# 256 rows of a weight matrix loaded in blocks of 80 and 16 partitions, with two permutation matmuls

## The chip, the core and the metric

The kernel runs on one core of one Trainium2 chip. The metric is the device time of one execution in microseconds (us). Engines are named as in the profile: PE (TensorE matmul), PEld (TensorE weight load), DVE (VectorE), ACT (ScalarE), POOL (GpSimd), SP (SyncE, which issues nearly all transfers). Sixteen DMA engines move the data.

## The reference, cut to what matters

One token passes a grouped-query attention over a long cache and, beside it, a gated feed-forward block; a sigmoid gate mixes the two.

```python
q = x @ wq                                  # x: 512, wq: 512 x 4096, 32 heads of 128
p = softmax(q . k_cache * 128**-0.5)        # 8 groups of 4 heads, 32768 keys of 128
a = (p @ v_cache) @ wo                      # wo: 4096 x 512
b = (silu(x @ w_gate) * (x @ w_up)) @ w_down    # w_gate, w_up: 512 x 1792; w_down: 1792 x 512
g = sigmoid((x * gate_w).sum())
out = g * a + (1 - g) * b
```

The two caches are 134 of the 148 MB that the kernel reads (8 x 32768 x 128 x 2 bytes each); everything is bf16.

## The kernel before

**Transfers.** SP issues one list of transfers in a fixed order (lines 317 to 348): wq, x and gate_w, w_gate and w_up; then the caches in pages of 4 MB (a page is one half of one group's keys or values: 128 partitions, 32 KB each), into four page buffers, each issued as soon as its buffer is free (waits at lines 307 and 312); then w_down in one transfer of 128 partitions with 14 KB each (line 343, tile `wd`); then wo in five transfers (line 338), cut by `WO_CUTS = [0, 8, 18, 26, 30, 32]` into 8, 10, 8, 4 and 2 blocks of 128 rows. Each ends by raising a semaphore of its own by 16.

**Start.** PE turns x and gate_w into columns (line 357; DVE copies them at 570 and 571), makes q from wq (370), permutes it (381), and makes the two feed-forward products from w_gate and w_up (394): 14 columns (`FC = 14`) of 128 values for each, four matmuls per column, into columns of the PSUM tile `ps_m`. Column j, partition p is feature 14 p + j, so the weight is read with a step of 14 elements. ACT and DVE make of it `tT` (520, 609, 613): 128 x 14, feature 14 p + j at partition p, which is the order in which `wd` has the rows of w_down.

**Loop over the eight groups.** PE transposes K pages (408), DVE copies the result to SBUF (630), PE makes the scores (420), DVE their maxima (635), ACT the exponentials (535), PE the sums over values (465).

**End** (`emit_end`, lines 475 to 498, and 673 to 691). PE sums the exponentials' sums (477, into `ps_e`); DVE takes the reciprocal (653), scales it (655) and, through a matmul with a permutation (491), makes `O2`, the attention output as 32 columns (668). `emit_wide` (205) multiplies one column with one 128 x 512 block, into one of four rows of the PSUM tile `ps_w`: 8 blocks of w_down, then 8 of wo (the first cut), the other 6 of w_down, and 10 of wo (the second cut). DVE copies `ps_w` to `part` (685). `emit_rows` (217) adds the four rows of `part`, and the other 14 blocks of wo, in four matmuls of 128 columns each. DVE writes `res_row` (687), and two small stores on SP and ACT (244) end the kernel.

Of the kernel before, what the change touches and what calls it, by code (L numbers as in the profile page):

```python
# [8 lines left out]
BF16 = mybir.dt.bfloat16  # L9
# [4 lines left out]
def bass_gated_mix__gqa_block_cached__swiglu_ffn__decode_kernel(  # L14
# [17 lines left out]
    H = A_wq.shape[1] // DH  # L32
    HPG = H // G
    F = B_w_gate.shape[1]
# [1 line left out]
    assert DH == 128 and D % 128 == 0 and F % 128 == 0 and HPG == 4 and NOUT == 512  # L36
    assert H == 32 and G >= 2
    KC = D // 128
    FC = F // 128

    R = 128
    BLK = 128 * R
# [13 lines left out]
    SCALE = float(DH) ** -0.5  # L56
    assert UPG == STEP == 4 * HPG and UPP % NKT == 0 and UPP % NST == 0
    assert KC * H * DH <= PAGE and 2 * KC * F <= PAGE and WOJ * NOUT <= PAGE
    WO_CUTS = [0, 8, 18, 26, 30, 32]
    KW = 1  # L60
    WD_CUT = 8
    WIDE = WO_CUTS[KW + 1]
# [3 lines left out]
    NSTRIP = 4  # L66
# [10 lines left out]
    with ExitStack() as es:  # L77
# [8 lines left out]
        sem_ld_wd = S_("s_ld_wd")  # L86
# [7 lines left out]
        sem_ident = S_("s_ident")  # L94
# [8 lines left out]
        sem_dve_x = S_("s_dve_x")  # L103
# [4 lines left out]
        sem_dve_tT = S_("s_dve_tT")  # L108
# [21 lines left out]
        def T(name, shape, dt):  # L130
            return es.enter_context(nc.sbuf_tensor(name, shape, dt))
# [6 lines left out]
        ident_f = T("ident_f", [128, 128], FP32)  # L138
        perm = T("perm", [128, 2, 128], BF16)
        pmat = T("pmat", [128, 128], BF16)  # L140
        xT = T("xT", [128, KC], BF16)
        gwT = T("gwT", [128, KC], FP32)
        prod_col = T("prod_col", [128, KC], FP32)
# [7 lines left out]
        sg = T("sg", [128, FC], FP32)  # L151
        t1 = T("t1", [128, FC], FP32)
        tT = T("tT", [128, FC], BF16)
        wd = T("wd", [128, FC, NOUT], BF16)
        page = T("page", [128, NPG, PAGE], BF16)
        ktT = T("ktT", [128, NKT, 2 * UW], BF16)
# [15 lines left out]
        O2 = T("O2", [128, WOJ], BF16)  # L172
# [9 lines left out]
        ps_m = P("ps_m", [128, 512], FP32)  # L182
# [3 lines left out]
        M_G0 = M_Q0 + H  # L186
        M_U0 = M_G0 + FC
        M_O0 = M_U0 + FC
# [11 lines left out]
        wgu = page[:, PG_F, 0 : 2 * KC * F].rearrange("p (w c f) -> p w c f", w=2, c=KC)  # L200
        wo_v = page[:, PG_X, 0 : WOJ * NOUT].rearrange("p (j n) -> p j n", j=WOJ)

        def emit_wide(pe, w, vec, j, first, last):
            c = j % NSTRIP
            return pe.matmul(  # L205
                ps_w[32 * c : 32 * c + 1, :],
                vec[:, j : j + 1],
                w[:, j, :],
                start=first,
                stop=last,  # L210
                skip_group_check=True,
            )
# [14 lines left out]
        def emit_wo(pe, k):  # L227
            pe.wait_ge(sem_wo[k], 16)
            for j in range(WO_CUTS[k], WO_CUTS[k + 1]):
                if j < WIDE:  # L230
                    ins = emit_wide(pe, wo_v, O2, j, False, j >= WIDE - NSTRIP)
                else:
                    ins = emit_rows(
                        pe,
                        lambda e: O2[:, j : j + 1] if e else O2z[:, j - WIDE, :],
                        wo_v[:, j, :],
                        False,
                        j == WOJ - 1,
                    )
            return ins  # L240
# [8 lines left out]
        with nc.Block("main") as block:  # L249
            @block.gpsimd  # L250
            def _(pool):
                pool.memset(ones_bf[:, :], 1.0).then_inc(sem_const, 1)
                pool.memset(ones_f[:, :], 1.0).then_inc(sem_const, 1)
                npool = [0]

                def chain(ins):
                    ins.then_inc(sem_pool, 1)
                    npool[0] += 1
                    pool.wait_ge(sem_pool, npool[0])

                pool.load_library(library_config.all_libraries[1])

                def ones_where(t, base, pattern):
                    return pool.affine_select(
                        out=t,
                        in_=t,
                        compare_op=ALU.not_equal,
                        fill=1.0,
                        base=base,
                        pattern=pattern,  # L270
                        channel_multiplier=1,
                    )

                pool.memset(ident[:, :], 0.0)
                pool.memset(ident_f[:, :], 0.0)
                pool.memset(perm[:, :, :], 0.0)
                pool.memset(sel5[:, :], 0.0)
                chain(pool.memset(pmat[:, :], 0.0))
                ones_where(ident[:, :], 0, [[-1, 128]]).then_inc(sem_ident, 1)
                ones_where(ident_f[:, :], 0, [[-1, 128]]).then_inc(sem_ident, 1)  # L280
                for e in range(2):
                    ones_where(perm[:, e, :], -e, [[0, 2], [-2, 64]]).then_inc(sem_ident, 1)
                ones_where(pmat[:, :], 0, [[-1, 32], [-32, 4]]).then_inc(sem_ident, 1)
                for c in range(NSTRIP):
                    chain(ones_where(sel4, -32 * c, [[-1, 16]]))
                pool.sem_inc(sem_ident, 1)
                pool.wait_ge(sem_dve_gpart, 1)
                pool.partition_all_reduce(gtot[:, :], gpart[:, :], 128, ReduceOp.add).then_inc(
                    sem_gtot, 1
                )  # L290
                for g in range(G):
                    pool.wait_ge(sem_pmax, STEP * (g + 1))
                    pool.partition_all_reduce(  # L293
                        gmax[:, g, :], pmax[:, g * STEP : g * STEP + HPG], 128, ReduceOp.max
                    ).then_inc(sem_gmax, 1)

            @block.sync
            def _(sp):
# [36 lines left out]
                def load_wo(k):  # L335
# [4 lines left out]
                load_v(G - 1, 0)  # L340
                sp.wait_ge(sem_fill, UPG * (G - 1) + UPP)
                cache(A_v_cache, G - 1, 1, PG_K[0], sem_page[PG_K[0]])
                sp.dma_start(  # L343
                    wd[:, :, :], B_w_down.rearrange("(p j) n -> p j n", j=FC)
                ).then_inc(sem_ld_wd, 16)
                sp.wait_ge(sem_pe_q, 1)
                for k in range(len(sem_wo)):
                    load_wo(k)
# [2 lines left out]
            def _(pe):  # L351
# [10 lines left out]
                            stop=True,  # L362
                        )
                ins.then_inc(sem_pe_x, 1)
                pe.wait_ge(sem_dve_x, 2)

                pe.wait_ge(sem_q, 16)
                for h in range(H):
# [6 lines left out]
                            stop=(c == KC - 1),  # L375
                        )
                ins.then_inc(sem_pe_q, 1)
                pe.wait_ge(sem_ident, 6)
                pe.wait_ge(sem_dve_qT, 1)
                for e in range(2):  # L380
                    ins = pe.matmul(
# [9 lines left out]
                for w, base in enumerate((M_G0, M_U0)):  # L391
                    for j in range(FC):
                        for c in range(KC):
                            ins = pe.matmul(  # L394
                                ps_m[:, base + j : base + j + 1],
                                wgu[:, w, c, :].rearrange("d (p j) -> d j p", j=FC)[:, j, :],
                                xT[:, c : c + 1],
                                start=(c == 0),
                                stop=(c == KC - 1),
                            )  # L400
# [73 lines left out]

                def emit_end():
                    pe.wait_ge(sem_dve_esum2, 1)
                    pe.matmul(  # L477
                        ps_e[:, 0:H],
                        ones_f[:, :],
                        esum2[:, :, :].rearrange("p g h -> p (g h)"),  # L480
                        start=True,
                        stop=True,
                    ).then_inc(sem_pe_S, 1)
                    emit_reduce((G + 1) * STEP)
                    pe.wait_ge(sem_dve_tT, 1)
                    pe.wait_ge(sem_ld_wd, 16)
                    pe.wait_ge(sem_psw, 1)
                    for j in range(WD_CUT):
                        emit_wide(pe, wd, tT, j, j < NSTRIP, False)
                    pe.wait_ge(sem_dve_oT2, 1)  # L490
                    pe.matmul(
                        ps_m[:, M_O0 : M_O0 + WOJ], pmat[:, :], O2a[:, :], start=True, stop=True
                    ).then_inc(sem_pe_O2, 1)
                    pe.wait_ge(sem_dve_O2, 1)
                    for k in range(KW):
                        emit_wo(pe, k)
                    for j in range(WD_CUT, FC):
                        emit_wide(pe, wd, tT, j, False, False)

                with pe.Fori(0, (G + 1) * STEP, STEP) as i:  # L500
                    for b in range(NB):
# [56 lines left out]
            def _(dve):  # L558
# [8 lines left out]
                dchain(dve.memset(qblk[:, :], 0.0))  # L567
                dve.sem_inc(sem_rc, 2 * STEP)
                dve.wait_ge(sem_pe_x, 1)
                dve.tensor_copy(xT[:, :], ps_m[:, M_X0 : M_X0 + KC]).then_inc(sem_dve_x, 1)  # L570
                dve.tensor_copy(gwT[:, :], ps_m[:, M_X0 + KC : M_X0 + 2 * KC]).then_inc(
                    sem_dve_x, 1
                )
                dve.wait_ge(sem_dve_x, 2)
                dve.tensor_tensor(prod_col[:, :], xT[:, :], gwT[:, :], ALU.mult).then_inc(
                    sem_dve_prod, 1
                )
# [44 lines left out]
                def copy_red(i, at):  # L622
                    dve.wait_ge(sem_red, i)
                    dve.tensor_copy(oT[:, at], ps_m[:, M_P0 : M_P0 + HPG]).then_inc(sem_rc, STEP)

                with dve.Fori(0, G * STEP, STEP) as i:
# [27 lines left out]
                dchain(  # L654
                    dve.tensor_scalar(rSg[:, :], rS[:, :], g_col[:, 0:1], None, op0=ALU.mult)
                )
                copy_red((G + 1) * STEP, slice((G + 1) * STEP, (G + 1) * STEP + HPG))
                dve.wait_ge(sem_rc, STEP * (G + 2))
                dve.tensor_tensor(
# [60 lines left out]
```

## Time and profile before

| | us |
|---|---|
| median of 3 runs (lowest to highest) | 351.55 (351.51 to 351.67) |
| the profiled execution: its own time | 351.52 |
| the profiled execution: span from first to last instruction | 350.2 |

| engine | busy us | share of the span |
|---|---|---|
| PE | 269.0 | 77% |
| PEld | 230.9 | 66% |
| DVE | 176.8 | 50% |
| ACT | 32.3 | 9% |
| POOL | 6.9 | 2% |
| DMA, SP's queue (q1) | | 98.6% of 16 engines' span, 148.12 MB |

Times inside an execution are counted from the start of the span. The profile has, beside busy times, a row of 40 slices for each engine (a digit is the busy share in tenths), the chain of work that ended last, followed back from the last instruction, and the groups of instructions with the mean time of one. The trace also has a record of each DMA packet: its queue, start, duration and bytes, but not the number of the DMA engine that ran it.

### The profile page before, as it was taken

How to read it: one execution, taken by the hardware profiler on the slowest of the kernel's cores; microseconds unless marked ns; L12 is line 12 of the kernel's file. 1: busy time of each engine (PE TensorE's matmuls, PEld its weight loads, DVE VectorE, ACT ScalarE, POOL GpSimd, SP SyncE). 2: the span in 40 equal slices, each digit the busy share in tenths (PEclk: the TensorE clock that was granted, in tenths of full speed). 3: DMA queues.
4: the chain of work that ended last, by engine and by line, in shares of the span. 5: the costliest groups of instructions: out<-in, count | busy, mean ns of one | idle time of the engine just before them, and what ended most of it. 6: DMA issues, size and time to landing. Idle time of an engine off the chain costs nothing.

```text
span 350.2 us, 8919 instructions
## 1 busy us (share of the span) xinstructions
PE 269.0 (77%) x4005; PEld 230.9 (66%) x4005; DVE 176.8 (50%) x193; ACT 32.3 (9%) x148; POOL 6.9 (2%) x29
## 2 busy tenths in 40 slices
PE   0446987799999959897797969694896949795675
PEld 0446987787796939495785839392886849493332
DVE  0111868474783928366382828183473819184011
ACT  1000000500030040002100040004000040004000
POOL 4000000000000000000000000000000000000000
PEclk9999989696998989679696969899698969679565
DMA  8999999999999999999999999999999999999995
GB/s 348 395 453 417 438 445 425 418 419 449 434 430 423 427 446 430 430 423 423 449 430 434 419 434 438 434 430 419 442 438 434 423 423 442 438 434 419 425 415 234
DMA packets 5924, 148.23 MB, mean 423 GB/s; under 512 B 666, under 2 KB 668, under 8 KB 924
## 3 DMA queue, kind: packets, MB, share of 16 engines
q1 hardware_dynamic: 5912, 148.12, 98.6%
q8 instruction: 6, 0.10, 0.1%
q14 instruction: 2, 0.02, 0.0%
q10 hardware_dynamic: 4, 0.00, 0.0%
HBM read 148.11 MB, written 0.00 MB: 423 GB/s over the span
## 4 chain that ended last, share of the span: by engine, by line
DMA 64%; PE 32%; DVE 2%; SPq 1%; issue 1%
DMA page<-in_A_k_cache_dram 53%; PE pst L408 24%; DMA page<-in_A_wo_dram 11%; PE ps_sc L420 5%; DVE ktT L630 1%; PE ps_o L465 1%; PE pst L217 1%; PE pst L205 0%; PE ps_m L446 0%; SPq L321 0%; SPq L300 0%; DVE part L685 0%; SPq L343 0%; SPq L338 0%; SPq L317 0%
## 5 line engine op out<-in xcount | busy, mean ns | idle before, releaser
L630 DVE COPY ktT<-pst 128x2048 bf16<-128x2048 bf16 x128 | 156.1, 1224 | 106.4 <-PE pst L408 99.2
L408 PE MATMUL pst<-ident_f,page 128*128 128x128 f32 x1024 | 158.8, 313 | 40.9 <-DMA page<-in_A_k_cache_dram 35.6
L408 PEld LDWEIGHTS pst<-ident_f,page 128*128 128x128 f32 x1024 | 136.1, 163 | 51.6 <-DMA page<-in_A_k_cache_dram 43.7
L420 PE MATMUL ps_sc<-qcur,ktT 128*128 128x8 bf16 x2048 | 67.8, 166 | 8.6 <-DVE ktT L630 8.6
L420 PEld LDWEIGHTS ps_sc<-qcur,ktT 128*128 128x128 bf16 x2048 | 66.9, 97 | 11.3 <-DVE ktT L630 10.0
L465 PE MATMUL ps_o<-page,ET 128*16 128x512 bf16 x512 | 43.2, 497 | 4.6 <-DMA page<-in_A_v_cache_dram 4.6
L465 PEld LDWEIGHTS ps_o<-page,ET 128*16 128x16 bf16 x512 | 13.5, 105 | 23.8 <-issue 11.9
L526 ACT ACTIVATE nbias<-gmax 128x4 f32<-128x4 f32 x8 | 1.7, 207 | 263.4 <-POOL gmax L293 263.4
L535 ACT ACTIVATE ET<-ps_sc,nbias 128x128 bf16<-128x128 f32 x64 | 24.1, 553 | 0.6
L535 ACT ACTIVATION_READ_ACCUMULATOR ET<-ps_sc,nbias 128x1 f32 x64 | 18.0, 282 | 0.0
L635 DVE TENSOR_REDUCE pmaxf<-ps_sc 128x4 f32<-128x512 f32 x16 | 11.1, 692 | 11.5 <-PE ps_sc L420 11.5
L446 PE MATMUL ps_m<-sel,acc 128*128 128x4 f32 x72 | 10.4, 268 | 3.8 <-ACT acc L547 3.8
L446 PEld LDWEIGHTS ps_m<-sel,acc 128*128 128x128 f32 x72 | 9.8, 211 | 4.4 <-ACT acc L547 4.4
L394 PE MATMUL ps_m<-xT,page 128*128 128x1 bf16 x112 | 6.9, 198 | 5.0 <-DMA page<-in_B_w_up_dram 5.0
L357 PE MATMUL ps_m<-ones_bf,x_row 1*128 1x1 bf16 x4 | 0.3, 172 | 12.9 <-DMA gw_row<-in_gate_w_dram 12.9
L394 PEld LDWEIGHTS ps_m<-xT,page 128*128 128x128 bf16 x112 | 6.8, 159 | 5.1 <-DMA page<-in_B_w_up_dram 5.1
L293 POOL PARTITION_ALL_REDUCE gmax<-pmax x8 | 3.0, 373 | 302.8 <-DVE pmax L637 302.8
L357 PEld LDWEIGHTS ps_m<-ones_bf,x_row 1*128 1x128 bf16 x4 | 0.2, 115 | 12.9 <-DMA gw_row<-in_gate_w_dram 12.9
L547 ACT ACTIVATE acc<-ps_o 128x512 f32<-128x512 f32 x8 | 5.2, 648 | 13.7 <-PE ps_o L465 13.7
L653 DVE RECIPROCAL rS<-pst 128x32 f32<-128x32 f32 x1 | 0.4, 357 | 12.0 <-PE pst L477 12.0
L570 DVE CAST xT<-ps_m 128x4 bf16<-128x4 f32 x1 | 0.2, 162 | 11.8 <-PE ps_m L357 11.8
L609 DVE TENSOR_TENSOR t<-sg,ps_m 128x14 f32<-128x14 f32 x1 | 0.2, 170 | 10.8 <-ACT sg L520 10.8
(65 smaller groups left out, 38.5 us busy)
## 6 DMA issues: line engine op xcount, KB each, us to landing
page<-in_A_k_cache_dram SPq DMA_DIRECT2D x16, 4096.0 KB, 27.1
page<-in_A_v_cache_dram SPq DMA_DIRECT2D x16, 4096.0 KB, 31.2
page<-in_A_wq_dram SPq DMA_DIRECT2D x1, 4096.0 KB, 12.2
page<-in_A_wo_dram SPq DMA_DIRECT2D x2, 1024.0 KB, 38.8
page<-in_B_w_gate_dram SPq DMA_DIRECT2D x1, 1792.0 KB, 15.3
page<-in_B_w_up_dram SPq DMA_DIRECT2D x1, 1792.0 KB, 20.5
wd<-in_B_w_down_dram SPq DMA_DIRECT2D x1, 1792.0 KB, 34.5
page<-in_A_wo_dram SPq DMA_DIRECT2D x1, 1280.0 KB, 39.1
```

The source lines that it names most:

```text
L217: ins = pe.matmul(ps_c[32 * oc : 32 * oc + (1 if e else SW), 0:128], lhs(e), rhs[:, oc * 128 : (oc + 1) * 128], start=first, stop=last, sk ...
L293: pool.partition_all_reduce(gmax[:, g, :], pmax[:, g * STEP : g * STEP + HPG], 128, ReduceOp.max).then_inc(sem_gmax, 1)
L394: ins = pe.matmul(ps_m[:, base + j : base + j + 1], wgu[:, w, c, :].rearrange("d (p j) -> d j p", j=FC)[:, j, :], xT[:, c : c + 1], start= ...
L408: ins = pe.transpose(pst[u % NST][:, k * 128 : (k + 1) * 128], kv[:, n * 128 : (n + 1) * 128], ident_f[:, :],)
L420: ins = pe.matmul(ps_sc[b][:, col : col + 2 * HPG], kt[:, k, e, :], qcur[:, e, :], start=(e == 0), stop=(e == 1),)
L446: ins = pe.matmul(ps_m[:, M_P0 : M_P0 + HPG], acc[:, q, :], sel4[:, q * HPG : (q + 1) * HPG], start=(q == 0), stop=(q == RQ - 1),)
L465: ins = pe.matmul(ps_o[32 * c : 32 * c + RQ * HPG, :], ET[:, n : n + RQ, :].rearrange("p n h -> p (n h)"), view[:, k * RQ : (k + 1) * RQ, ...
L526: act.activation(nbias[:, g, :], gmax[:, g, :], ACT.Copy, scale=-SCALE).then_inc(sem_nbias, 1)
L535: act.activation(ET[:, b * R : (b + 1) * R, h], sc[:, h, :], ACT.Exp, bias=nbias[:, g, h : h + 1], scale=SCALE, accum_out=esum[:, g, b, h ...
L547: act.activation(acc[:, :, :].rearrange("p q d -> p (q d)"), ps_o[:, :], ACT.Copy).then_inc(sem_acc, STEP)
L630: dve.tensor_copy(ktT[:, u % NKT, :], pst[u % NST][:, :].bitcast(BF16)).then_inc(sem_cp, 1)
L635: dve.tensor_reduce(pmaxf[:, b, :], sc, AX.X, ALU.max).then_inc(sem_pmax, 4)
```

## The change

The 1792 features are cut in another way. The first 1536 keep the old form with 12 columns (feature 12 p + j). The other 256 form three columns of 80 features and one of 16, so there are 16 columns in place of 14. w_down is loaded in three transfers: 128 partitions x 12 KB; 80 partitions x 3 KB; 16 partitions x 1 KB. In the last two, the rows are put in an order in which the outermost dimension of the source is 10 and 2: partition p = 8 e + i has the rows of r = 10 i + e (e below 10, i below 8), and in the small one p = 8 e + i has r = 2 i + e.

`tT` has these features in plain order, r at partition r. So two matmuls with permutation matrices (`pmx`, made by POOL) bring the last four columns into the order of the rows; DVE copies the result from PSUM to a new tile `tX`. DVE also sets to zero, at the start, the 32 columns of `ps_m` that the feed-forward products go to, and PE waits for that before it goes on. The wait for `tT` moves ahead of the first matmul of `emit_end`. The second cut of wo has 11 blocks in place of 10 and the third 7 in place of 8.

```diff
-    FC = F // 128
+    FW, FX = 12, 3
+    XP, XE, XL = 8, 10, 2
+    FN = [128] * FW + [XE * XP] * FX + [XL * XP]
+    FC = len(FN)
+    F1 = FW * 128
+    F2 = F1 + FX * XE * XP
...
-    WO_CUTS = [0, 8, 18, 26, 30, 32]
+    WO_CUTS = [0, 8, 19, 26, 30, 32]
...
+        def ffn_cols(w, c, j):
+            v = wgu[:, w, c, :]
+            if j < FW:
+                return v[:, 0:F1].rearrange("d (p j) -> d j p", j=FW)[:, j, :]
+            if j < FW + FX:
+                return v[:, F1:F2].rearrange("d (r b) -> d b r", b=FX)[:, j - FW, :]
+            return v[:, F2:F]
...
+                pool.memset(pmx[:, :], 0.0)
...
+                for e, at in ((XE, 0), (XL, XE * XP)):
+                    ones_where(pmx[:, at : at + e * XP], 0, [[-1, e], [-e, XP]]).then_inc(
+                        sem_ident, 1
+                    )
...
-                sp.dma_start(
-                    wd[:, :, :], B_w_down.rearrange("(p j) n -> p j n", j=FC)
-                ).then_inc(sem_ld_wd, 16)
+                for dst, src in (
+                    (wd[:, 0:FW, :], B_w_down[0:F1, :].rearrange("(p j) n -> p j n", j=FW)),
+                    (
+                        wd[0 : XE * XP, FW : FW + FX, :],
+                        B_w_down[F1:F2, :].rearrange("(i e b) n -> e i b n", i=XP, b=FX),
+                    ),
+                    (
+                        wd[0 : XL * XP, FC - 1, :],
+                        B_w_down[F2:F, :].rearrange("(i e) n -> e i n", i=XP),
+                    ),
+                ):
+                    sp.dma_start(dst, src).then_inc(sem_ld_wd, 16)
...
-                pe.wait_ge(sem_dve_x, 2)
+                pe.wait_ge(sem_dve_x, 3)
...
-                pe.wait_ge(sem_ident, 6)
+                pe.wait_ge(sem_ident, 8)
...
-                                ps_m[:, base + j : base + j + 1],
-                                wgu[:, w, c, :].rearrange("d (p j) -> d j p", j=FC)[:, j, :],
+                                ps_m[0 : FN[j], base + j : base + j + 1],
+                                ffn_cols(w, c, j),
...
                     pe.wait_ge(sem_dve_esum2, 1)
+                    pe.wait_ge(sem_dve_tT, 1)
+                    for j, n, at in ((FW, FX, 0), (FW + FX, 1, XE * XP)):
+                        m = FN[j]
+                        pe.matmul(
+                            ps_e[0:m, H + j - FW : H + j - FW + n],
+                            pmx[0:m, at : at + m],
+                            tT[0:m, j : j + n],
+                            start=True,
+                            stop=True,
+                        )
...
-                    pe.wait_ge(sem_dve_tT, 1)
-                    pe.wait_ge(sem_ld_wd, 16)
+                    pe.wait_ge(sem_ld_wd, 48)
...
                     for j in range(WD_CUT, FC):
-                        emit_wide(pe, wd, tT, j, False, False)
+                        vec = tT[:, j : j + 1] if j < FW else tX[0 : FN[j], j - FW : j - FW + 1]
+                        emit_wide(pe, wd, vec, j, False, False)
...
+                dve.memset(ps_m[:, M_G0:M_O0], 0.0).then_inc(sem_dve_x, 1)
                 dve.tensor_copy(xT[:, :], ps_m[:, M_X0 : M_X0 + KC]).then_inc(sem_dve_x, 1)
...
+                dve.tensor_copy(tX[:, :], ps_e[:, H : H + FX + 1])
                 copy_red((G + 1) * STEP, slice((G + 1) * STEP, (G + 1) * STEP + HPG))
```

`emit_wide` now takes a column of fewer than 128 partitions too, and uses as many partitions of the block.

More of the change, by code (lines that the diff above doesn't have):

```diff
@@ L38, in bass_gated_mix__gqa_block_cached__swiglu_ffn__decode_kernel @@
     KC = D // 128
-    FC = F // 128
+    FW, FX = 12, 3
[4 more added lines that the diff above has]
+    F2 = F1 + FX * XE * XP
+    assert sum(FN) == F
     R = 128
@@ L140, in bass_gated_mix__gqa_block_cached__swiglu_ffn__decode_kernel @@
         pmat = T("pmat", [128, 128], BF16)
+        pmx = T("pmx", [128, (XE + XL) * XP], BF16)
         xT = T("xT", [128, KC], BF16)
@@ L153, in bass_gated_mix__gqa_block_cached__swiglu_ffn__decode_kernel @@
         tT = T("tT", [128, FC], BF16)
+        tX = T("tX", [128, FX + 1], BF16)
         wd = T("wd", [128, FC, NOUT], BF16)
@@ L201, in bass_gated_mix__gqa_block_cached__swiglu_ffn__decode_kernel @@
         wo_v = page[:, PG_X, 0 : WOJ * NOUT].rearrange("p (j n) -> p j n", j=WOJ)
+        def ffn_cols(w, c, j):
[5 more added lines that the diff above has]
+            return v[:, F2:F]
         def emit_wide(pe, w, vec, j, first, last):
             c = j % NSTRIP
+            n = vec.shape[0]
             return pe.matmul(
                 ps_w[32 * c : 32 * c + 1, :],
-                vec[:, j : j + 1],
-                w[:, j, :],
+                vec,
+                w[0:n, j, :],
                 start=first,
@@ L230, in emit_wo @@
                 if j < WIDE:
-                    ins = emit_wide(pe, wo_v, O2, j, False, j >= WIDE - NSTRIP)
+                    ins = emit_wide(pe, wo_v, O2[:, j : j + 1], j, False, j >= WIDE - NSTRIP)
                 else:
@@ L484, in emit_end @@
                     emit_reduce((G + 1) * STEP)
-                    pe.wait_ge(sem_dve_tT, 1)
-                    pe.wait_ge(sem_ld_wd, 16)
+                    pe.wait_ge(sem_ld_wd, 48)
                     pe.wait_ge(sem_psw, 1)
                     for j in range(WD_CUT):
-                        emit_wide(pe, wd, tT, j, j < NSTRIP, False)
+                        emit_wide(pe, wd, tT[:, j : j + 1], j, j < NSTRIP, False)
                     pe.wait_ge(sem_dve_oT2, 1)
@@ L573, in _ @@
                 )
-                dve.wait_ge(sem_dve_x, 2)
+                dve.wait_ge(sem_dve_x, 3)
                 dve.tensor_tensor(prod_col[:, :], xT[:, :], gwT[:, :], ALU.mult).then_inc(
```

## The prediction

> **What bounds the kernel now.** I read the page first: DMA row, queue shares, then the chain of work that ended last.
>
> ```profile
> DMA  8999999999999999999999999999999999999995
> q1 hardware_dynamic: 5912, 148.12, 98.6%
> q8 instruction: 6, 0.10, 0.1%
> q14 instruction: 2, 0.02, 0.0%
> ...
> DMA 64%; PE 32%; DVE 2%; SPq 1%; issue 1%
> ```
>
> The DMA engines are busy from start to end: the kernel is as long as its transfers and a short tail. So a gain or a loss must show in when the last transfer lands, or behind it. The chain from 340 us, in order of time (start, us, what), tells what the tail is:
>
> ```profile
> 343.70 0.04 issue
> 343.74 1.46 PE pst L205 x10
> 345.20 0.02 issue
> 345.23 0.70 DVE part L685
> 345.93 0.04 issue
> 345.97 2.11 PE pst L217 x52
> 348.09 0.03 issue
> 348.12 0.43 PE pst L217 x4
> 348.55 0.02 issue
> 348.58 0.29 DVE res_row L687
> ```
>
> PE starts at 343.74, just after the second cut of wo has landed (343.70 by its semaphore), and the last four of its matmul records start at 348.12, just after the last cut (348.07). After that come 0.46 us of PE, 0.29 of DVE and the stores. The waits of this stretch agree (engine, for whom, us, times): PE stood idle for wo three times.
>
> ```profile
> PEld pst L205 <- DMA page<-in_A_wo_dram: 2.5, 1, 2.5
> ...
> PEld pst L217 <- DMA page<-in_A_wo_dram: 0.6, 2, 0.3
> ```
>
> The decisive view is the DMA row from 344 to 349 us, in 40 slices of 0.125 us:
>
> ```profile
> DMA  9999799898899965554444433422000000000000
> ```
>
> Until about 345.8 all engines run (nines and eights); then six to five tenths of them have work, then four, until 347.5. The transfers end unevenly. To see who is late I followed the trace's packet records. On a running engine the next packet starts 3 to 4 ns before the record of the one before ends, and every transfer of 128 partitions gives eight packets and a 4-byte semaphore write to each of sixteen engines (384 packets of 14336 B are three transfers of 128). Joined by these two rules, they form sixteen streams without a gap:
>
> ```
> engines  packet on another queue                               last packet ends
> 8        none                                                  345.79 to 345.99
> 1        q14, 8 KB at 131.06                                   346.37
> 1        q14, 8 KB at 64.50                                    346.86
> 6        q8, 16 KB at 19.20 31.60 44.09 51.23 59.78 66.81      347.30 to 347.66
> ```
>
> Up to such a packet the streams lie within 0.5 us of each other. A 16 KB instruction packet takes 1.00 to 1.11 us, the packet behind it 0.5 us more than its like, so its engine is 1.5 us late from then on; an 8 KB one costs 0.7 to 1.0. Nothing gives this back, since no stream ever waits. A landing's semaphore stands 0.41 us behind the last packet (347.66 to 348.07). **So the bound is the slowest of six engines delayed by one instruction fetch each;** the mean of the sixteen ends is 346.55, 1.1 us earlier, and that is all that any balancing could win.
>
> **The change part by part.** *The three transfers of w_down.* Before, each engine gets 8 packets of 14336 B. After, each gets 8 of 12288 B. The share of the other two depends on how a transfer is dealt out. Rows: outermost dimension 128, sixteen engines; the two stores, outermost 2, two packets on two engines each; x and gate_w, outermost 1, one packet on one engine, an engine of the eight early ones. By these rows, 10 gives ten engines with 8 packets of 3072 B, and 2 gives two with 8 of 1024 B. Six engines get neither. Durations by size: 2048 B 0.084 us, 4096 B 0.159, 8192 B 0.312, 10240 B 0.387, 14336 B 0.535, 1024 B 0.046. Between neighbours that gives 12288 B 0.461 and 3072 B 0.122; a step from packet to packet is 3 ns less. So:
> - six engines: 8 x (0.532 - 0.458) = 0.59 us less;
> - ten engines: 8 x 0.119 + 0.006 - 0.59 = 0.36 more;
> - two of the ten: a further 8 x 0.043 + 0.006 = 0.35, so 0.71 more.
>
> Which engines are late the records don't say, since they name none. No view ties the six to a side; for the forecast I take it that the six that are spared are the six late ones. For it: the engine that took the one-packet transfers is an early one; the six instruction packets fell on six different engines, as if in turn, so a run of six neighbours is natural. Then the ends are: late 347.66 - 0.59 = 347.07; the two with 8 KB packets 346.86 + 0.36 = 347.22 and 346.73; the two with most 346.70 at most; the other six 346.35 at most. The latest is 347.22, **0.44 us earlier**. Ends of the range: 0.59 if those two didn't count, and +0.71 if a late engine is one of the two with most.
>
> [...]
>
> *Two cuts of wo.* The second cut is 8 x 1024 B larger per engine, 0.30 us, the third as much smaller. The second lands at 343.70 - 0.44 + 0.30 = 343.56. Its eleven matmuls go, as the ten do, in groups of four, so DVE starts part 1.48 us later as now, at 345.08, and PE the rows at 345.82. 8 matmul records for part, 0.27 us, then 28 for the third cut (landed 345.76) at 0.92/32 = 0.029 each: done at 346.89. The fourth cut lands at 346.99, the fifth at 347.63: PE still waits for both, so the end follows the last landing and the whole 0.44 is kept. The cover is 0.1 us; with 32 matmuls in place of 28 it would be gone.
>
> *Start.* The zeroing of 128x32 by DVE delays xT by something like the CAST of 0.16 us (bounds: nothing, and 0.48, the 128x512 memset); wq's matmuls end that much later, but PE then idles 5.0 us for w_up. PE has 16 more feed-forward matmuls at 6.88/112 = 0.061 each, 1.0 us (less if a smaller step loads faster: the wq ones, without a step, take 0.028). PE ends them at 30.6 instead of 29.65, ACT and DVE 0.8 later, and the first K page is there at 32.45: hidden, with 1 us left. POOL's one memset (0.21) and two selects (0.3 to 0.5) end near 6 us; PE needs them at 17.5. SP's two more issues, at 0.43 each and perhaps twice that, delay wo's from 304 to 305 or 306; the streams reach wo near 335.8. All nothing.
>
> *End.* Two more matmuls ahead of the one at 477 (0.19 each by the row of 491, between 0.1 and 0.3) push the chain to O2 from 340.31 to 340.7 or so; DVE's copy to tX (0.16 to 0.19) falls in its idle 0.76 us before 339.40. Two more blocks of w_down: 0.3. PE is then done with them near 342.9 in place of 342.2, and wo's second cut lands at 343.56. Hidden; 0.65 us of cover is left.
>
> **Sum**, against the profiled execution: 351.52 - 0.44 = **351.1** (its own time lies 0.03 from the median of 351.55, and 1.3 above its span of 350.2). That is 0.13%.
>
> **The rivals.**
> - *B, a spared six, but the 346.86 engine is one of the two with most:* 346.86 + 0.71 = 347.57, 0.09 earlier: 351.4. Two places in ten at most, and one of them is taken by an undisturbed engine if the one-packet transfers go to one of these two.
> - *C, late engines among the ten:* their end becomes 347.66 to 348.02 (+0.00 to +0.36): 351.5 to 351.9; on one of the two with most, up to 352.2. For: nothing in the profile names the engines. [...] Against C: six are late and six are spared, and the one engine that the records do mark, by the one-packet transfers, is on the side that C needs full of late ones and is not late.
> - *D, slower:* a seventh instruction packet. PE's program grows by 17 matmuls and their weight loads, and its instructions come in blocks of 16 KB; if that makes one more block, one more engine loses 1.55 us. It decides only where it falls on an engine that is already late: 347.66 - 0.59 + 1.55 = 348.62, +0.96, 352.5; on an early engine the end is 345.99 + 0.36 + 1.55 = 347.90, still same. Against: 17 on top of 832 in the listing is 2%, and the last packet came at 66.8 us, though the code of the end ran at 337.
> - *E, faster:* PE had a clock of 0.50 in the stretch 343.00 to 350.20; granted in full, the 0.46 and 1.46 us of PE behind landings would be shorter by up to half. Only the 0.46 counts: 0.44 + 0.23 = 0.67, 350.85.
> - *The change doesn't do what it says:* the last transfers are dealt evenly to sixteen engines; then all get the bytes of before and the time is 351.5 (in C).
>
> **How the numbers follow.** A measurement of this kernel can tell about 0.2%, 0.70 us, from no change. Chances: forecast 0.58 (own range 350.9 to 351.3), B 0.07, C 0.23, D 0.07, E 0.05. Eight in ten: from the forecast's lower end to the upper end of C but for its worst place, 350.9 to 351.9. Within 0.2%: forecast, B and C, 0.88; slower: D, 0.07; faster: E and what I don't see, 0.05.
>
> **What would show it.** Right: the DMA row at the end falls later than now from its nines, and steeply; the streams without instruction packets end near 346.3, six late ones near 347.07; the five cuts land by 0.4 earlier except the second. Wrong: streams with 16 KB packets end after 347.66; a seventh packet on q8; PE no longer waits for the fourth and fifth cut.

## The result, and the profile after

The changed kernel takes 353.62 us (median of 6 runs, 353.37 to 353.96); the kernel before, on the same chip, 351.59 (6 runs, 351.51 to 351.67). The ratio is 1.0058, 95% interval 1.0045 to 1.0071: **2.0 us slower**, where 0.44 us faster was forecast. The profiled execution took 353.85, its span is 352.4.

The page of the changed kernel, the same lines as before:

```profile
DMA  8999999999999999999999999999999999999995
...
q1 hardware_dynamic: 6020, 148.12, 98.5%
q8 instruction: 7, 0.11, 0.1%
q14 instruction: 2, 0.02, 0.0%
...
DMA 64%; PE 31%; DVE 2%; SPq 1%; issue 0%
```

Busy to the end as before, with the same bytes, and one instruction packet more on q8. The page alone shows no reason. The chain from 340 us (start, us, what) shows where the time is:

```profile
306.47 39.72 DMA page<-in_A_wo_dram
346.18 0.04 issue
346.23 1.47 PE pst L222 x11
347.70 0.02 issue
347.72 0.70 DVE part L728
348.43 0.04 issue
348.47 1.82 PE pst L234 x48
350.29 0.00 issue
350.29 0.44 PE pst L234 x4
350.73 0.02 issue
350.75 0.29 DVE res_row L730
```

The tail has the shape that it had: 1.47, 0.70, rows, 0.44, 0.29. It starts later: the second cut of wo landed at 346.18 in place of 343.70, the last at 350.25 in place of 348.07. That is 2.2 us, all of the difference of the spans. w_down itself landed at 340.55 in place of 338.12, and PE stood idle 1.4 us for it, a wait that the kernel before doesn't have; it is hidden, since the second cut of wo comes at 346.18. PE still waits for wo (waits of the stretch from 338 us):

```profile
PE pst L222 <- DMA page<-in_A_wo_dram: 2.1, 2, 1.2
...
PEld pst L234 <- DMA page<-in_A_wo_dram: 0.3, 1, 0.3
```

The DMA row from 346 to 352 us, 40 slices of 0.15 us:

```profile
DMA  9699999898986554321110000003000000000000
```

The nines end near 348 in place of 345.8, and then it falls through 6, 5, 4 to 1: the streams now end one after the other over some 3 us. (The 3 alone is the seventh instruction packet, at 350.17, behind all data.) Where did the 2 us arise? The busy times by stretch, with the granted clock, the DMA share and GB/s in the last three columns, first of the kernel before:

```profile
335.00:337.00 2.00, 2.00 (x24) 0.60 (x16) 0.00 (x0) 0.00 (x0) 0.00 (x0) 0.50 0.92 387
337.00:339.00 2.00, 1.76 (x17) 1.26 (x10) 0.60 (x2) 0.60 (x1) 0.00 (x0) 0.81 1.02 424
```

and of the changed kernel:

```profile
333.00:335.00 2.00, 0.92 (x12) 0.36 (x16) 0.00 (x0) 0.00 (x0) 0.00 (x0) 0.50 1.00 424
335.00:337.00 2.00, 2.00 (x28) 0.62 (x20) 0.00 (x0) 0.00 (x0) 0.00 (x0) 0.52 1.06 272
337.00:339.00 2.00, 1.80 (x20) 1.38 (x12) 0.76 (x3) 0.60 (x1) 0.00 (x0) 1.00 0.98 268
339.00:341.00 2.00, 0.58 (x10) 0.18 (x9) 0.57 (x3) 0.00 (x0) 0.00 (x0) 0.83 0.99 370
341.00:343.00 2.00, 0.84 (x13) 0.22 (x9) 0.31 (x2) 0.00 (x0) 0.00 (x0) 0.50 1.05 443
```

From 335 to 339 us, while w_down's two small transfers run, the engines are as "busy" as ever (1.06 and 0.98) and move 272 and 268 GB/s in place of 387 and 424. So in these rows a full DMA share is not the full rate: 1.06 goes with 272 GB/s here, 1.02 with 424 before. The packet records (mean us of one, behind 325 us of the execution):

```
bytes   before   after
14336   0.539    -
12288   -        0.517   (0.464 until 335 us)
 3072   -        0.194   (0.121 the shortest)
 1024   -        0.066
 8192   0.314    0.419   (first cut of wo)
11264   -        0.428   (second cut of wo)
```

The excess over the usual durations (0.461, 0.122, 0.046 and 0.314) adds up to 7.2 (12288 B) + 5.8 (3072 B) + 0.3 (1024 B) + 13.4 (first cut of wo) = 26.7 us, 1.67 for each of sixteen streams, and the mean of the streams' ends moved by about as much, from 346.55 to 348.25. Three quarters of it fell on packets other than the small ones. All sixteen streams were slowed together, by a mean factor in each half microsecond of 1.5, 1.8, 1.9, 1.8, 1.5, 1.4, 1.6, 1.4 and 1.3 from 335.5 to 340, then none; single packets lay between 1.0 and 2.8.

### The profile page after: what moved, and what is told of

It is laid out like the page before. It is cut to its first block, busy times and chain, and to the rows that moved or that the text cites. A ratio compares the mean times of both kernels' runs of the same rounds, so it can differ in the third digit from the quotient of the medians.

```text
span 352.4 us, 8963 instructions
## 1 busy us (share of the span) xinstructions
PE 271.7 (77%) x4022; PEld 231.6 (66%) x4022; DVE 176.9 (50%) x195; ACT 32.3 (9%) x148; POOL 7.4 (2%) x32
## 4 chain that ended last, share of the span: by engine, by line
DMA 64%; PE 31%; DVE 2%; SPq 1%; issue 0%
DMA page<-in_A_k_cache_dram 53%; PE pst L439 22%; DMA page<-in_A_wo_dram 11%; PE ps_sc L451 5%; PE ps_o L496 2%; DVE ktT L672 2%; PE pst L234 1%; SPq L376 1%; PE pst L222 0%; PE ps_m L477 0%; SPq L343 0%; SPq L322 0%; DVE part L728 0%; SPq L360 0%; SPq L339 0%
## 5 line engine op out<-in xcount | busy, mean ns | idle before, releaser
L425 PE MATMUL ps_m<-xT,page 128*128 128x1 bf16 (+2 forms) x128 | 7.9, 198 | 4.9 <-DMA page<-in_B_w_up_dram 4.9
L425 PEld LDWEIGHTS ps_m<-xT,page 128*128 128x128 bf16 (+2 forms) x128 | 7.8, 162 | 5.1 <-DMA page<-in_B_w_up_dram 5.0
```

What stands on the lines that cost most here:

```text
L425: ins = pe.matmul(ps_m[0 : FN[j], base + j : base + j + 1], ffn_cols(w, c, j), xT[:, c : c + 1], start=(c == 0), stop=(c == KC - 1),)
```

## The experiments

Three theories of what slows the packets. **Place of writing:** each engine has places of its own, the partitions that it writes in a transfer of 128, and in the change most of an engine's partitions are other engines' places, so two or more engines write to one place. This is the author's conjecture: the packet records hold neither an engine nor a partition, so no run shows whose place a partition is, or that two writes meet. What the runs can show is at which partitions a transfer is slow. **Place of reading:** ten engines read neighbouring 3 KB pieces of one 30 KB stretch of memory. **Small packets:** 3 KB and 1 KB packets are slow by their size or number. The diffs below show the lines that matter, with `...` for the others (semaphore counts, sizes that follow).

### Neither of the small transfers

```diff
-   wd[0 : XE * XP, FW : FW + FX, :],
-   wd[0 : XL * XP, FC - 1, :],
...
+   dve.memset(wd[:, FW:FC, :], 0.0)
```

> The changed kernel without its two small transfers (256 rows of w_down are not loaded; zeros stand in their place, so the output lacks them). If the loss of 2.0 us comes from the two transfers, every packet has its usual length, each stream ends 0.59 us earlier than in the kernel before (last packet near 347.1) and the time is about 351.0. If it comes from the other edits (the two matmuls, the cuts of wo, the longer feed-forward stage), the streams end early but the time stays above 352.5.

351.21 us, ratio 0.9987 (0.9977 to 0.9996). Every packet has its usual length (12288 B: 0.464; 8192 B: 0.314), and the last ends at 347.41. That is later than the 347.1 expected: the streams end 0.58 earlier on the mean, but the last of the late ones only 0.25. So the other edits cost nothing, and the whole loss comes from the two transfers.

### Dealt to sixteen engines

```diff
-   B_w_down[F1:F2, :].rearrange("(i e b) n -> e i b n", i=XP, b=FX)
+   B_w_down[F1:F2, :].rearrange("(r b) n -> r b n", b=FX)
-   B_w_down[F2:F, :].rearrange("(i e) n -> e i n", i=XP)
+   B_w_down[F2:F, :]
-   ones_where(pmx[:, at : at + e * XP], 0, [[-1, e], [-e, XP]])
+   ones_where(pmx[:, at : at + e * XP], 0, [[-1, e * XP]])
```

> The changed kernel, with the 240 and the 16 rows in natural order: the same 3 KB and 1 KB packets, but 80 partitions dealt to sixteen engines with 5 each, and 16 with 1 each (the permutations become identities). Theory 'place of reading' (ten engines read neighbouring 3 KB pieces of one 30 KB stretch at the same time, and that slows every reader): the pieces of two engines now lie 15 KB apart, packets take 0.12 us, time 351.6. Theory 'place of writing' (an engine's partitions are those of other engines' shares in the 128-partition transfers, so two engines write to one place): 5 partitions in a row cross such borders too, packets stay at 0.17 to 0.22, time 352.5 to 353.6. Theory 'small packets' (3 KB and 1 KB packets are slow by their size): 353.6.

353.13 us, ratio 1.0037 (1.0023 to 1.0052); 3 KB packets 0.184 on the mean. Ten engines are not the point: the same rows on sixteen lose 1.4 us, within what "place of writing" forecast.

### Reading far apart

```diff
-   B_w_down[F1:F2, :].rearrange("(i e b) n -> e i b n", i=XP, b=FX)
+   B_w_down[0 : XE * 104, :].rearrange("(e q) n -> e q n", e=XE)[:, 0:96, :]
+       .rearrange("e (i b) n -> e i b n", b=12)[:, :, 0:FX, :]
```

(and the small one in the same way)

> The changed kernel, with the two small transfers reading rows that lie far apart: the engines 104 KB from each other, the pieces of one engine 12 KB from each other; ten and two engines, sizes and partitions as in the change (the rows are others, so the output is not the reference's). 'Place of reading': packets of 3 KB take 0.12 us, the last stream ends near 347.7, time 351.6. 'Place of writing' and 'small packets': packets of 0.17 to 0.22 us and all sixteen streams at half speed for some 4 us as in the change, time 353.6.

353.41 us, ratio 1.0049 (1.0032 to 1.0066); 3 KB packets 0.186. The same stretches:

```profile
335.00:337.00 2.00, 2.00 (x24) 0.75 (x20) 0.00 (x0) 0.00 (x0) 0.00 (x0) 0.50 1.09 282
337.00:339.00 2.00, 2.00 (x15) 1.20 (x7) 0.36 (x1) 0.60 (x1) 0.00 (x0) 0.50 0.95 263
```

282 and 263 GB/s as in the change: "place of reading" falls.

### Four partitions for each of ten engines

```diff
-   wd[0 : XE * XP, FW : FW + FX, :],
-   B_w_down[F1:F2, :].rearrange("(i e b) n -> e i b n", i=XP, b=FX)
+   wd[0 : XE * 4, FW : FW + FX, :],
+   B_w_down[F1 : F1 + 120, :].rearrange("(i e b) n -> e i b n", i=4, b=FX)
...
```

> The changed kernel, with 40 partitions x 3 KB in place of 80 (half of the 240 rows are left out, so the output lacks them): ten engines with 4 partitions each, same 3 KB packets, ten neighbours in a 30 KB stretch as in the change. [...] 'Place of reading' and 'small packets': packets of 0.17 to 0.22, about half of the loss, time 352.4 to 352.8.

351.53 us, ratio 0.9990 (0.9980 to 1.0000); 3 KB packets 0.130 on the mean. The stretches:

```profile
335.00:337.00 2.00, 2.00 (x24) 0.60 (x16) 0.00 (x0) 0.00 (x0) 0.00 (x0) 0.50 0.99 343
337.00:339.00 2.00, 1.84 (x19) 1.23 (x11) 0.76 (x3) 0.60 (x1) 0.00 (x0) 0.86 1.03 427
```

Packets of the same size, ten engines, neighbouring pieces, and the slow spell shrinks to about one microsecond near 336: 343 GB/s from 335 to 337 us, 427 behind it. "Place of reading" and "small packets" expected 352.4 to 352.8. It supports "place of writing", but half of the bytes are gone, so the next pair leaves all of them in.

### The kernel before with w_down in halves: by partitions, and by columns

```diff
-   sp.dma_start(wd[:, :, :], B_w_down.rearrange("(p j) n -> p j n", j=FC))
+   for lo in (0, 64):
+       sp.dma_start(wd[lo : lo + 64, :, :],
+                    B_w_down.rearrange("(p j) n -> p j n", j=FC)[lo : lo + 64, :, :])
```

```diff
+   for lo in (0, 7):
+       sp.dma_start(wd[:, lo : lo + 7, :],
+                    B_w_down.rearrange("(p j) n -> p j n", j=FC)[:, lo : lo + 7, :])
```

> The kernel before, with w_down loaded in two transfers of 64 partitions in place of one of 128; packets (14336 B), rows and their order in memory are the same, each still on sixteen engines with 4 partitions each. [...] 'Small packets' and 'place of reading': nothing changes but one more issue, 351.6. [...]

> Counterpart of the halves: the kernel before, with w_down loaded in two transfers of 128 partitions with 7 KB each. 'Place of writing': each engine keeps its partitions, packets of 7168 B take 0.275 us, time 351.6. 'Small packets', or a cost of each further transfer: the time rises by what such packets or a transfer cost, 351.8 to 353.

By partitions: 357.81 us, ratio 1.0175 (1.0160 to 1.0191), 6.1 us slower, with the same 14336 B packets at 1.02 us on the mean. By columns: 351.92, ratio 1.0005 (0.9996 to 1.0015), 7168 B packets at 0.276; the 0.2 us above the kernel before can't be told from nothing. Halves by partitions:

```profile
333.00:335.00 2.00, 0.00 (x0) 0.00 (x0) 0.00 (x0) 0.00 (x0) 0.00 (x0) 0.50 0.95 201
335.00:337.00 2.00, 1.80 (x20) 0.68 (x24) 0.00 (x0) 0.00 (x0) 0.00 (x0) 0.50 0.99 237
337.00:339.00 2.00, 2.00 (x22) 0.59 (x13) 0.00 (x0) 0.11 (x1) 0.00 (x0) 0.53 0.98 208
339.00:341.00 2.00, 1.25 (x10) 1.04 (x9) 0.84 (x4) 0.48 (x1) 0.00 (x0) 1.00 0.99 206
341.00:343.00 2.00, 0.00 (x0) 0.00 (x0) 0.33 (x2) 0.00 (x0) 0.00 (x0) 0.82 0.93 183
```

Half the rate for some ten microseconds, with large packets and rows read as always: "small packets" falls too. Packets of w_down at twice their 0.535 us would make 8 x 0.53 = 4.3 us, by estimate; the loss is above that, since the streams that were already at wo, in transfers of 128 partitions, ran at half speed as well (8192 B packets mostly at 1.9 to 2.1 times their usual 0.312, single ones up to 3.2).

### The small transfer alone

Diff: as with neither, but with the 16-row transfer.

> The changed kernel with the 16-row transfer but without the 240 rows (zeros in their place, so the output lacks them): how much of the loss comes from two engines with 8 packets of 1 KB. [...] 'Small packets': two early engines end 0.35 later and nothing else changes, 351.2.

351.42 us, ratio 0.9992 (0.9982 to 1.0001), beside 351.21 without it. 1 KB packets 0.049 on the mean (0.046 is usual), and in no half microsecond are the packets longer than 1.05 times their usual on the mean; single 8192 B ones reach 1.2. It hardly slows the others, and the two intervals overlap: it can't be told whether 0.2 us is its price. The loss is the 240 rows'.

### The same idea on partitions 0 to 31

```diff
-    FW, FX = 12, 3
-    XP, XE, XL = 8, 10, 2
-    FN = [128] * FW + [XE * XP] * FX + [XL * XP]
+    FW, FX = 13, 4
+    XP, XE = 4, 8
+    FN = [128] * FW + [XE * XP] * FX
...
+   wd[0 : XE * XP, FW : FW + FX, :],
+   B_w_down[F1:F, :].rearrange("(i e b) n -> e i b n", i=XP, b=FX)
```

> The idea of the change without the foreign partitions: 13 columns of 128 features and 4 of 32; 128 rows go to 32 partitions in the order that gives eight engines four partitions each, 4 packets of 4 KB; all 256 rows are used. 'Place of writing': no packet is longer than usual; eight engines get 0.30 us less, eight 0.33 more than before. If the six engines delayed by 16 KB instruction packets are all among the eight spared, the last packet ends 0.30 earlier and the time is 351.3; if one is not, it ends where it did, 351.6. 'Small packets': 4 KB packets were never slow, so the same. 'Place of reading' (eight engines read neighbouring 4 KB pieces of a 32 KB stretch): packets of 0.25 to 0.3 us in place of 0.16 and a loss of 1 us, 352.5.

351.71 us, ratio 0.9999 (0.9990 to 1.0008). No packet is longer than usual (4096 B: 0.161). The loss is gone, and nothing is gained, as the expectation has it for one late engine that is not spared: of the six streams with 16 KB packets five were spared (ends 346.95 to 347.56) and the sixth, with its packet at 63.1 us, was among the eight with more; its last packet ends at 347.66, where the last one ended before. In this execution that is not all: one of the five spared ends at 347.56, so with the sixth spared too only 0.1 us would have been won.

### The same, at other partitions

```diff
-   wd[0 : XE * XP, FW : FW + FX, :]
+   wd[PX : PX + XE * XP, FW : FW + FX, :]     # PX = 32, or 64
```

(the second operand and the permutation's output moved along)

> The kernel with eight engines and four partitions each (128 rows on 32 partitions), with these at partitions 32 to 63 in place of 0 to 31; rows, packets and engines are the same. [...] If every partition range other than 0 to 31 collides (a place is one group of four partitions): two writers per place for about 1.3 us, streams at half speed meanwhile, 352.3 to 352.7.

> The same with partitions 64 to 95. [...] If only the partitions' number or the dealing to ten engines mattered in the change, nothing happens: 351.7.

At 32 to 63: 351.75 us, ratio 0.9999 (0.9989 to 1.0008); here the five spared streams end by 347.25 and the sixth alone at 347.70. At 64 to 95: 352.99, ratio 1.0036 (1.0024 to 1.0048), above the 352.3 to 352.7 that the expectation for 32 to 63 gives for partitions that collide. Its 4 KB packets of w_down took 0.224 us on the mean in place of 0.160, and the 8192 B packets of the first cut of wo 0.398 in place of 0.314. Same rows, same engines, same packets, other partitions. At 32 to 63:

```profile
335.00:337.00 2.00, 2.00 (x24) 0.58 (x16) 0.00 (x0) 0.00 (x0) 0.00 (x0) 0.50 0.99 413
337.00:339.00 2.00, 1.69 (x15) 1.27 (x11) 0.76 (x3) 0.60 (x1) 0.00 (x0) 0.95 1.01 421
```

At 64 to 95:

```profile
335.00:337.00 2.00, 2.00 (x24) 0.65 (x20) 0.00 (x0) 0.00 (x0) 0.00 (x0) 0.50 1.01 299
337.00:339.00 2.00, 1.93 (x14) 1.15 (x6) 0.55 (x2) 0.60 (x1) 0.00 (x0) 0.50 1.00 307
```

This pair is the clearest support for "place of writing": only the partitions differ in it, and 64 to 95 cost 1.2 us more than 32 to 63 (352.99 and 351.75). What sets the two ranges apart was not shown.

### Four engines

Diff: as on partitions 0 to 31, but `XP, XE = 4, 4`, and two transfers of 16 partitions, at 0 and at 32.

> The same 128 rows dealt to four engines in place of eight: two transfers of 16 partitions, at 0 to 15 and 32 to 47, four packets of 4 KB each for engines 0 to 3. Twelve engines end 0.30 us earlier than in the kernel before, four 0.95 later; no packet is longer than usual if 0 to 15 and 32 to 47 are these engines' own places. If neither of the engines with instruction packets at 63 to 67 us (one 16 KB, one 8 KB; both were among the eight) is among the four, the last packet ends 0.30 earlier: 351.3. If one of them is, it ends 0.5 to 0.6 later than in the kernel before: 352.2.

351.80 us, ratio 1.0001 (0.9992 to 1.0010). No packet is longer than usual. The stream with the 8 KB packet at 63.4 was one of the four and ends last, at 347.93; the twelve others end by 347.69. Neither case of the expectation fits in size, but its rule does: a late stream among those with more. No version better than the kernel before was found.

## Why the prediction was wrong

- **What bounds the kernel: right.** The last landing sets the end before and after; the tail behind it moved as one piece.
- **How the transfers are dealt: right.** The streams of the changed kernel have 8 packets of 3072 B on ten engines and 8 of 1024 B on two of these; six have neither.
- **The step that failed: "Between neighbours that gives 12288 B 0.461 and 3072 B 0.122".** It took the durations from packets that nothing slowed, and it took every other packet as unchanged. The durations were right where nothing is slowed (0.464 and, the shortest, 0.121). But 3072 B packets took 0.194 us on the mean, and while they ran, the packets of all sixteen streams took 1.3 to 1.9 times their usual on the mean of a half microsecond. That is 1.67 us for each stream; the prediction had nothing for it, in no rival and in neither end of its range.
- **"The six that are spared are the six late ones": five of six.** The stream with the sixth 16 KB packet, at 63.3 us, was among the ten. By itself that would have been the forecast's rival C: if it is the stream of the sixth packet before, at 66.81, 347.31 + 0.36 = 347.67, no change. In the changed kernel this stream ends last, at 349.76. That engines are fewer is not what cost the 2.0 us: sixteen engines lost 1.4, and eight on partitions 0 to 31 nothing.
- **Rival D, slower by a seventh instruction packet:** the packet came (seven on q8), but at 350.17, behind all data; it costs nothing. The other sign of being wrong came too, all six streams with 16 KB packets ending after 347.66 (348.26 to 349.76). They did so because of the slowed packets, which no rival had.
- **The rest held.** DVE's zeroing took 0.09 us; the feed-forward matmuls 7.92 in place of 6.88, and PE then still idled 1.81 before the first K page; the permutation's copy to tX lies in DVE's idle time; wo's second cut came long after O2. The kernel without the two transfers shows it all at once: 351.21.

By the runs, then: the two small transfers lose 2.0 us by slowing the packets of all sixteen streams, and by the pair at 32 and at 64 it is the partitions written that decide. At partitions 0 to 31 and 32 to 63, where no packet is slowed, the balance alone is left, and it gains nothing (351.71 and 351.75), since one late engine is on the wrong side.

Left open: whether two engines that write to one place are the cause, and why a transfer on some engines slows all sixteen. Between 338.5 and 339.5 us only one stream of the changed kernel was still at its 3 KB packets, and the other fifteen, in a transfer of 128 partitions, took 1.2 to 1.8 times their usual. The runs show that it is so, not the path by which it happens. Open too is which engine an instruction packet falls on: the records name none.

## What to carry to other kernels

Before a transfer is cut to fewer than 128 partitions, measure it at the partitions that it is to write. Here transfers of 80 partitions cut the rate of all sixteen engines to about two thirds (272 and 268 GB/s in place of 387 and 424) and halves of 64 to about a half (183 to 237), also for those busy with something else, while the DMA share stayed near 1. Thirty-two partitions on eight engines cost nothing at 0 to 31 and at 32 to 63, and 1.2 us at 64 to 95; halves by columns, all 128 partitions in each, cost nothing that can be told. Read GB/s or packet durations beside the busy share. And before bytes are moved away from late engines, find out which engines are late: here instruction packets of 1.0 to 1.1 us decide it, and an idea that was right for five of six gained nothing.

## What the runs showed of the hardware that was not expected

- The five of six are no accident of one execution. In all six kernels with a transfer on eight or ten engines, the streams joined from the packet records show the sixth 16 KB packet, and both 8 KB ones, on engines with more, and the first five 16 KB packets on spared engines.
- A further transfer as such cost nothing on the engines: w_down in two halves by columns, 1.0005 (0.9996 to 1.0015).
- SP's issues were held up, for a reason that the runs don't show. With w_down in three transfers the fourth and fifth cut of wo took 10.0 and 8.5 us to issue, in place of 0.43 each; the issues of wo in the two kernels, before and changed:

```profile
304.12 2.33 SPq L338 DMA_DIRECT2D page<-in_A_wo_dram  x5
```

```profile
306.01 19.90 SPq L360 DMA_DIRECT2D page<-in_A_wo_dram  x5
```

The streams reach wo only near 336, so it cost nothing; halves by columns have 13.69 us there and lose nothing.
